# A third buffer for rows of q and k, and new slots for their loads: a threshold attention followed by a gated two-layer network

## Chip, cores and metric

One core of one Trainium2 chip. The metric is the device time of one launch in microseconds (us), as the median of several runs; the profile is of one execution of the same program.

## What is computed

Inputs are q, k and v of shape (8, 8, 576, 64) in f32 (batch, head, row, head dimension), a number tau, and two weight matrices, 512 x 2048 and 2048 x 512.

```python
scores = q @ k.T / 8
scores = where(scores >= rowmax(scores) - tau, scores, -1e9)
attn = exp(scores - rowmax(scores)); attn = attn / (sum(attn) + 1e-9)
x = (attn @ v)              # heads side by side: (4608, 512)
h = x @ w_in                # (4608, 2048)
out = (h * clip(h + 3, 0, 6) / 6) @ w_out
```

## The kernel before, in words

**Units.** The 64 heads are worked in 16 quads of four heads; a batch entry has two quads (g = 0, 1). A quad has nine slots: in slots 0 to 3 the first pair of heads, 128 rows at a time, in slots 4 to 7 the second pair, and in slot 8 the last 64 rows of all four heads. So there are 144 slots, numbered n = 0 to 143 (slot s of quad Q is n = 9Q + s), and one loop over n (lines 470 to 558) writes out by hand, for every engine, what is issued in each slot. The order of the program is the order on each engine and on each DMA queue; semaphores are added to it by the framework.

**What one slot does.** TensorE computes the scores of slot n + 1 (line 281, or 287 in slot 8). VectorE reads those of slot n out of PSUM and takes the row maxima (302). ScalarE masks (310) and, one slot later, takes the exponential and the row sums (315). GpSimd multiplies with the reciprocal sums and writes bf16 probabilities pn (323), also one slot later; in time this ends some seven to nine us after the slot's line 302 began. SyncE then issues a DMA transpose of pn (331) into pT (slots 0 to 7) or pR (slot 8). In the first 21 slots every odd one is transposed by TensorE instead (339). TensorE multiplies the transposed probabilities with v: `av_main` for the first pair in slot 8, `av_main` for the second pair in slot 3 of the next quad, `av_rest` for slot 8 in slot 4 of the next quad (348, 351). Beside this, from slot 23 on, each slot takes a piece of the two-layer network of an earlier batch entry (378, 387 or 389, 395, 407, 415), and finished output rows are stored by SyncE (428).

**Loads of q and k.** `load_quad` (80) takes tiles from `nat_pool` and appends five jobs to the list `loads`: k rows of the first pair, q rows of the first pair, the last 64 rows, k of the second pair, q of the second pair. The loop starts one job per slot (553), behind that slot's transpose on SyncE's queue. For batch entries 0 and 1 (quads 0 to 3) a k or q job is two DMAs (88), and TensorE transposes the rows. From quad 4 on a k or q job is four DMAs of 32-column blocks (97 and 92), the job of the last rows is two DMAs (124), and VectorE transposes (239, 245). Of quad Q + 1, q of the first pair is read in slot 5 of quad Q, k in slot 6, the last rows in slot 7; the second pair is read in slots 1 and 2 of its own quad. With two buffers quad Q + 2 may be loaded from slot 4 of quad Q on; that is where its jobs are appended (480). Quad 4 so falls to slots 22 to 26, quad 5 to 34 to 38, quad 6 to 40 to 44, quad 7 to 49 to 53, and each later quad nine slots after the one before it.

**Other loads.** Values of a batch entry (`load_v`, 133) are four casting DMAs issued by GpSimd from the list `vcasts`; the 32 casting DMAs of the weights stand in `casts` (156). Lines 554 to 557 say which list gets a turn in which slot: weights one per slot in slots 4 to 15, 20, 21 and 29 to 32, two per slot in 22 to 28; values of the second entry in 16 to 19, of the third in 34 to 37, and later ones as they are appended (slots 45, 63, 81, ...).

**Waits of SyncE.** All DMAs of SyncE's queue share eight completion semaphores in turn, so each DMA also waits for the one eight places before it. A transpose besides waits for its pn, a load for the readers of its buffer. What stands behind a waiting instruction of SyncE waits with it.

Of the kernel before, what the change touches and what calls it, by code (L numbers as in the profile page):

```python
# [21 lines left out]
def kernel(  # L22
# [17 lines left out]
    NQUAD = B * H // 4  # L40
# [5 lines left out]
    tau = float(tau)  # L46

    singles = ctx.enter_context(tc.tile_pool(name="singles", bufs=1))
    nat_pool = ctx.enter_context(tc.tile_pool(name="nat", bufs=2))
    v_pool = ctx.enter_context(tc.tile_pool(name="vp", bufs=2))  # L50
    qk_pool = ctx.enter_context(tc.tile_pool(name="qk", bufs=2))
    s_pool = ctx.enter_context(tc.tile_pool(name="sp", bufs=4))
# [15 lines left out]
    nat = {}  # L68
# [6 lines left out]
    casts = []  # L75
# [4 lines left out]
    def load_quad(quad):  # L80
        b, g = divmod(quad, 2)
        nat[quad] = (nat_pool.tile([P, 1152], F32, tag="nq", name="nq"),
                     nat_pool.tile([P, 4, 4, D], F32, tag="km", name="km"),
                     nat_pool.tile([P, 2 * D], F32, tag="kr", name="kr"))
        nq, km, kr = nat[quad]

        def main(dst, src, h, order, by=nc.sync):
            by.dma_start(out=dst[:, :, h, :], in_=src[b, 4 * g + h, 0:512, :].rearrange(order, t=4))

        def blocks_q(n, a, j):  # L90
            c = 32 * (2 * a + j)
            nc.sync.dma_start(out=nq[c:c + 32, n * S:(n + 1) * S].rearrange("p (k d) -> p k d", d=32),
                              in_=q[b, 4 * g + 2 * n + a, :, 32 * j:32 * j + 32].rearrange("(k r) d -> r k d", r=32))

        def blocks_k(n, a, j):
            c = 32 * (2 * a + j)
            nc.sync.dma_start(
                out=km[c:c + 32].rearrange("p t h d -> p (t h d)")[:, n * 512:(n + 1) * 512].rearrange(
                    "p (t m d) -> p t m d", t=4, d=32),
                in_=k[b, 4 * g + 2 * n + a, 0:512, 32 * j:32 * j + 32].rearrange("(m r t) d -> r t m d", r=32, t=4))  # L100

        def load_k(n):
            if b < NB:
                for a in range(2):
                    main(km, k, 2 * n + a, "(p t) d -> p t d")
            else:
                for a in range(2):
                    for j in range(2):
                        blocks_k(n, a, j)

        def load_q(n):
            if b < NB:
                for a in range(2):
                    main(nq[:, 0:1024].rearrange("p (t h d) -> p t h d", h=4, t=4), q, 2 * n + a, "(t p) d -> p t d",
                         by=nc.scalar if quad == n == 0 else nc.sync)
            else:
                for a in range(2):
                    for j in range(2):
                        blocks_q(n, a, j)

        def rest():
            for dst, src in ((kr[:], k), (nq[:, 1024:1152], q))[0:2 if b < NB else 1]:
                for n in range(2):
                    nc.sync.dma_start(out=dst[64 * n:64 * n + 64, :].rearrange("p (h d) -> p h d", h=2),
                                      in_=src[b, 4 * g + 2 * n:4 * g + 2 * n + 2, 512:S, :].rearrange("h p d -> p h d"))

        for n in range(2):
            loads.append(lambda n=n: load_k(n))
            loads.append(lambda n=n: load_q(n))
            if n == 0:  # L130
                loads.append(rest)

    def load_v(b):
        vm = v_pool.tile([P, H, 4 * D], BF16, tag="vm", name="vm")
        vr = vrs[b % 2]
        vsb[b] = (vm, vr)
        for g in range(2):
            vcasts.append(lambda g=g: nc.gpsimd.dma_start(
                out=vm[:, g * 4:g * 4 + 4, :],
                in_=v[b, g * 4:g * 4 + 4, 0:512, :].rearrange("h (p t) d -> p h (t d)", t=4)))  # L140
        for a in range(2):
            vcasts.append(lambda a=a: nc.gpsimd.dma_start(
                out=vr[a * 64:(a + 1) * 64, a, :, :],
                in_=v[b, :, 512:S, :].rearrange("(hp a) p d -> a p hp d", a=2)[a]))
# [21 lines left out]
    def start(jobs, n):  # L166
        for _ in range(min(n, len(jobs))):
            jobs.pop(0)()
# [144 lines left out]
    def sm_exp(sl, i):  # L313
        s = sl.s[:, i, :]
        nc.scalar.activation(out=s, in_=s, func=Act.Exp, accum_out=sl.rsum[:, i:i + 1])  # L315

    def sm_recip(sl):
        nc.vector.reciprocal(out=sl.rinv[:], in_=sl.rsum[:])  # L318
# [54 lines left out]
    def mm1(item, pool=None):  # L373
        b, ni, c0, w = item
        hps = (pool or ps_h).tile([P, 2, 512], F32, tag="s" if pool else "h", name="h")
        for n in range(2):
            for ki in range(KI):
                nc.tensor.matmul(hps[:, n, 0:w], w_in_sb[:, ki, (ni + n) * P:(ni + n + 1) * P],  # L378
                                 xT[b][:, ki, c0:c0 + w], start=(ki == 0), stop=(ki == KI - 1))
        return hps[:, :, 0:w]  # L380
# [89 lines left out]
    for n, sl in enumerate(queue):  # L470
        quad, slot = sl.quad, sl.slot
        b, g = divmod(quad, 2)
        now = n
        if slot in (0, 4):
            pts[2 * quad + slot // 4] = pt_pool.tile([P, 9, 512], BF16, tag="pT", name="pT")
        if slot == 8:
            ptr[quad] = ptr_pool.tile([P, 9, P], BF16, tag="pR", name="pR")
        if quad == 0 and slot == 0:
            load_quad(1)
        if slot == (4 if quad else 8) and quad + 2 < NQUAD:  # L480
            load_quad(quad + 2)
        if slot == 0 and g == 1 and b + 1 < B:
            load_v(b + 1)
        if prev is not None:
            for i in range(2):
                sm_exp(prev, i)
        sm_max(sl)

        if slot != 8 and todo1:
            item, then = todo1.pop(0)  # L490
            h = mm1(item)
            r = mm1_relu(h, on_act=(slot in ((1, 2, 3, 5, 6) if quad >= 2 * NB else (0, 1, 3, 5))))
            mm1_gate(item, h, r)
            todo2.extend(then)
        copies = pe_transpose(queue[n - 2]) if n > 1 and queue[n - 2].on_chip else None
        if prev is not None:
            sm_recip(prev)
        if copies:
            copies()
        outs = []  # L500


        pieces = 0 if slot == 3 else 1
        if slot == 0:
            second = True
        if second and slot < 2 and len(todo2) > 1 and todo2[0][1] == todo2[1][1]:
            pieces, second = 2, False
        for _ in range(pieces):
            if todo2:
                bb, mt, part = todo2.pop(0)  # L510
                mm2_part(bb, mt, part)
                if part == 3:
                    outs += mm2_out(bb, mt, on_act=False)
        for i in range(2):
            sm_mask(sl, i)
        evict = None
        nxt = 2 * quad + 2
        if slot == 1:
            evict = transpose_q(2 * quad + 1)
        elif slot == 2:  # L520
            evict = transpose_k(2 * quad + 1)
        elif n == 3:
            evict = transpose_rest(0, of_k=False)
        elif slot == 3 and quad > 0:
            av_main(2 * quad - 1)
        elif slot == 4 and quad > 0:
            av_rest(quad - 1)
            if quad % 2 == 0:
                todo1.extend(moe_of(quad // 2 - 1))
        elif slot in (5, 6, 7) and quad + 1 < NQUAD:  # L530
            if slot == 5:
                alloc_qk(quad + 1)
                evict = transpose_q(nxt)
            elif slot == 6:
                evict = transpose_k(nxt)
            else:
                evict = transpose_rest(quad + 1)
        elif slot == 8:
            av_main(2 * quad)
        if evict:  # L540
            evict()
        if n == 0:
            warm_up(8)
        if n + 1 < len(queue):
            queue[n + 1].tiles = scores(queue[n + 1].quad, queue[n + 1].slot)
        if n < 8:
            warm_up(6)
        if prev is not None:
            sm_norm(prev)
        flush()  # L550
        late.extend(outs)
        if not 30 < n < 34:
            start(loads, 1)
        if n < 4 or 15 < n < 20 or n > 33:
            start(vcasts, 1)
        elif n > 3:
            start(casts, 2 if 21 < n < 29 else 1)
        prev = sl

    for i in range(2):  # L560
# [78 lines left out]
```

## Time and profile before

| | |
|---|---|
| median of three runs | 549.75 us (549.46, 549.75, 554.11) |
| the profiled execution | 551.66 us, its span 549.9 us |
| granted TensorE clock, mean | 0.997 |
| TensorE matmul busy | 524.2 us, 95% |
| ScalarE, VectorE, GpSimd busy | 463.3 (84%), 429.1 (78%), 305.1 us (55%) |
| DMA queue of SyncE | 67.47 MB, 70.0% of the 16 engines' span |
| DMA queue of GpSimd | 8.92 MB, 13.8% |

Starts of line 302 show when slots begin. The first of a quad and the length of the quad, in us:

| quad | 0 | 1 | 2 | 3 | 4 | 5 | 6 | 7 | 8 |
|---|---|---|---|---|---|---|---|---|---|
| slot 0 begins | 9.5 | 35.2 | 60.7 | 88.2 | 123.0 | 155.1 | 187.0 | 216.9 | 248.4 |
| length | 25.7 | 25.6 | 27.4 | 34.8 | 32.1 | 31.9 | 29.9 | 31.5 | 31.2 |

In the profile PE is TensorE, PEld its weight loads, DVE VectorE, ACT ScalarE, POOL GpSimd, SP SyncE and SPq its queue of DMA issues; L12 is line 12. A timeline line gives start and length in us, engine, line, operation, output and input, how many instructions were merged, and in square brackets how long the engine had been idle and what ended that. A DMA issue's length is the time it held the issuing queue, not the transfer. A busy PE is not PE at its peak, since matmuls are pipelined.

### The profile page before, as it was taken

The page shows a single profiled execution, that of the slowest core. Times are in us where ns is not written, and L with a number is a line of the kernel's source. Part 1 is how long each engine was busy: PE and PEld are TensorE (multiplying, and loading weights), DVE is VectorE, ACT ScalarE, POOL GpSimd, SP SyncE. Part 2 cuts the span into 40 slices and gives each one's busy share as a digit, 9 for nine tenths or more (in the row PEclk, how much of TensorE's full clock was granted, in tenths as well). Part 3 has the DMA queues.
Part 4 walks back from the last instruction along what each step waited for, and adds up shares of the span by engine and source line. Part 5 has one row for each costly group of instructions (what it writes and reads, how often), then busy time and mean ns, then how long its engine had stood idle before and what let it go on. Part 6 is the DMA issues. An engine that isn't in the chain of part 4 may idle for free.

```text
span 549.9 us, 11477 instructions
## 1 busy us (share of the span) xinstructions
PE 524.2 (95%) x3733; PEld 300.5 (55%) x3774; DVE 429.1 (78%) x1055; ACT 463.3 (84%) x986; POOL 305.1 (55%) x646
## 2 busy tenths in 40 slices
PE   8999898899999999999999999999999999999997
PEld 7755455445545565555555555555555555554663
DVE  3788886688978888888989788888988788873441
ACT  3999989789989899899899899899888899993440
POOL 1888888665566555755566555754556555561000
PEclk9999999899999999999999999999999999999999
DMA  5999989969979788997789788988689785653102
GB/s 110 140 133 180 183 124 181 188 108 177 163 135 196 128 163 145 171 165 141 117 154 199 129 167 129 207 152 149 131 132 191 140 155 99 124 111 90 39 19 77
DMA packets 311692, 77.52 MB, mean 141 GB/s; under 512 B 294608, under 2 KB 307152, under 8 KB 311632
## 3 DMA queue, kind: packets, MB, share of 16 engines
q1 hardware_dynamic: 293024, 67.47, 70.0%
q0 software_dynamic: 17408, 8.92, 13.8%
q8 instruction: 30, 0.49, 0.4%
q10 hardware_dynamic: 1200, 0.39, 0.3%
q14 instruction: 30, 0.25, 0.2%
HBM read 36.70 MB, written 9.44 MB: 84 GB/s over the span
## 4 chain that ended last, share of the span: by engine, by line
PE 55%; ACT 10%; DVE 7%; DMA 5%; POOL 4%; issue 4%; SPq 1%; POOLq 0%; DVEq 0%
PE o L407 17%; PE h L378 16%; PE s L281 15%; ACT s L310 4%; PE av L348 4%; ACT s L315 3%; DVE s L302 3%; POOL pn L323 3%; DMA pR<-pn 3%; ACT r L387 2%; PE s L287 2%; DMA pT<-pn 2%; DVE g L395 1%; DVE r L389 1%; DMA km<-in_k_dram 1%
## 5 line engine op out<-in xcount | busy, mean ns | idle before, releaser
L323 POOL TENSOR_SCALAR pn<-s,rinv 128x576 bf16<-128x576 f32 x288 | 211.6, 745 | 126.7 <-DVE rinv L318 61.1
L302 DVE TENSOR_SCALAR_CACHE_REDUCE s<-s 128x576 f32<-128x576 f32 x288 | 205.3, 749 | 33.0 <-PE s L281 24.9
L310 ACT ACTIVATE s<-s,bias 128x576 f32<-128x576 f32 x288 | 206.9, 766 | 26.7 <-POOL bias L305 26.3
L315 ACT ACTIVATE s<-s 128x576 f32<-128x576 f32 x288 | 192.4, 670 | 0.3
L281 PE MATMUL s<-kT,qT 64*128 64x288 f32 x1024 | 172.8, 432 | 4.5 <-DVE s L302 4.2
L378 PE MATMUL h<-xT,w_in_sb 128*128 128x320 bf16 (+1 forms) x1024 | 145.8, 288 | 3.6 <-DVE g L395 2.2
L407 PE MATMUL o<-w_out_sb,g 128*128 128x512 bf16 x535 | 133.5, 379 | 6.0 <-DVE osb L415 3.7
L281 PEld LDWEIGHTS s<-kT,qT 64*128 64x128 f32 x1024 | 96.1, 186 | 65.9 <-DVE s L302 35.0
L378 PEld LDWEIGHTS <-w_in_sb 128*128 128x128 bf16 x1024 | 92.0, 98 | 66.9 <-issue 40.2
L395 DVE SCALAR_TENSOR_TENSOR g<-r,h 128x512 bf16<-128x512 f32 (+1 forms) x128 | 96.4, 754 | 37.2 <-ACT r L387 35.8
L305 POOL TENSOR_SCALAR bias<-m 128x1 f32<-128x1 f32 x288 | 54.4, 189 | 64.8 <-DVE s L302 44.7
L407 PEld LDWEIGHTS <-g 128*128 128x128 bf16 x576 | 55.6, 98 | 58.2 <-issue 9.7
L387 ACT ACTIVATE r<-h,three 128x640 f32<-128x640 f32 (+1 forms) x86 | 63.0, 733 | 27.0 <-PE h L378 26.6
L315 ACT ACTIVATION_READ_ACCUMULATOR s<-s 128x1 f32 x288 | 54.2, 188 | 0.0
L415 DVE TENSOR_SCALAR osb<-o 128x512 f32<-128x512 f32 x31 | 20.9, 675 | 21.7 <-PE o L407 21.4
L348 PE MATMUL av<-pT,vm 128*64 128x512 bf16 x256 | 33.7, 385 | 1.8 <-DMA pT<-pn 1.8
L348 PEld LDWEIGHTS <-vm 128*64 128x64 bf16 x512 | 17.6, 110 | 27.2 <-issue 15.8
L389 DVE TENSOR_SCALAR r<-h 128x512 f32<-128x512 f32 (+1 forms) x42 | 31.5, 750 | 0.3 <-PE h L378 0.3
L318 DVE RECIPROCAL rinv<-rsum 128x2 f32<-128x2 f32 x144 | 23.0, 160 | 8.4 <-ACT s L315 7.7
L360 DVE CAST xT<-av 128x512 bf16<-128x512 f32 x32 | 21.8, 681 | 6.5 <-PE av L351 6.5
L302 DVE DVE_READ_ACCUMULATOR s<-s 128x1 f32 x288 | 24.0, 83 | 0.0
L287 PE MATMUL s<-kT,qT 64*64 64x288 f32 x256 | 21.3, 415 | 0.6 <-DVE s L302 0.6
(57 smaller groups left out, 220.6 us busy)
## 6 DMA issues: line engine op xcount, KB each, us to landing
out_dram<-osb SPq DMA_DIRECT2D x31, 256.0 KB, 2.7
nq<-in_q_dram SPq DMA_DIRECT2D x96, 72.0 KB, 2.9
km<-in_k_dram SPq DMA_DIRECT2D x96, 64.0 KB, 2.6
vm<-in_v_dram POOLq DMA_DIRECT2D x16, 256.0 KB, 5.3
km<-in_k_dram SPq DMA_DIRECT2D x16, 128.0 KB, 3.7
w_in_sb<-in_moe_w_in_dram POOLq DMA_DIRECT2D x16, 128.0 KB, 4.1
w_out_sb<-in_moe_w_out_dram POOLq DMA_DIRECT2D x16, 128.0 KB, 4.2
pT<-pn SPq DMA_TRANSPOSE x119, 3.7
```

The costliest lines, as they stand in the source:

```text
L281: nc.tensor.matmul(tiles[a][:, hf, 0:HALF], qT_of(pair)[a * 64:(a + 1) * 64, t * P:(t + 1) * P], keys(pair, a, hf), start=True, stop=True)
L302: nc.vector.tensor_scalar(out=sl.s[:, i, :].rearrange("p (a b) -> p a b", a=2), in0=ps[:, :, 0:HALF], scalar1=1.0, scalar2=None, op0=Alu.m ...
L305: nc.gpsimd.tensor_scalar(out=sl.bias[:, i:i + 1], in0=sl.m[:, i:i + 1], scalar1=-scale, scalar2=tau, op0=Alu.mult, op1=Alu.add)
L310: nc.scalar.activation(out=s, in_=s, func=Act.Prelu, bias=sl.bias[:, i:i + 1], scale=scale, alpha=REJECT)
L315: nc.scalar.activation(out=s, in_=s, func=Act.Exp, accum_out=sl.rsum[:, i:i + 1])
L323: nc.gpsimd.tensor_scalar(out=pn[:, i, :], in0=sl.s[:, i, :], scalar1=sl.rinv[:, i:i + 1], scalar2=1.0, op0=Alu.mult, op1=Alu.mult)
L348: nc.tensor.matmul(ps[a * 64:(a + 1) * 64, :], vm[:, 2 * hp + a, c * D:(c + 1) * D], pT[:, 5 * a + c, cols], start=(c == 0), stop=False)
L378: nc.tensor.matmul(hps[:, n, 0:w], w_in_sb[:, ki, (ni + n) * P:(ni + n + 1) * P], xT[b][:, ki, c0:c0 + w], start=(ki == 0), stop=(ki == KI ...
L387: nc.scalar.activation(out=r, in_=hps, func=Act.Relu, bias=three[:])
L389: nc.vector.tensor_scalar(out=r, in0=hps, scalar1=3.0, scalar2=0.0, op0=Alu.add, op1=Alu.max)
L395: nc.vector.scalar_tensor_tensor(out=gbuf[:, ni:ni + 2, c0:c0 + w], in0=r, scalar=6.0, in1=hps, op0=Alu.min, op1=Alu.mult)
L407: nc.tensor.matmul(o_ps[0], gbuf[:, ni, mt * P:(mt + 1) * P], w_out_sb[:, ni, :], start=(ni == 0), stop=(ni == NI - 1))
```

## The change

`nat_pool` gets a third buffer, so a quad's rows may be loaded a quad earlier. Jobs of quads 1 and 2 are appended in slot 0, those of quad Q + 3 in slot 3 of quad Q. No job of `loads` starts in slots 20 to 35. By this rule quads 1 to 4 are loaded in slots 0 to 19 without a pause, quads 5 to 8 in slots 36 to 55 without a pause, quad 9 in slots 57 to 61, and each later quad in slots 3 to 7 of the quad three before it. Values of the third entry go to slots 32 to 35; weights go two per slot in slots 22 to 29 and end with slot 31. Orders of TensorE, VectorE and ScalarE are the same; on GpSimd only these casts move; SyncE has the same DMAs in another order.

```diff
-    nat_pool = ctx.enter_context(tc.tile_pool(name="nat", bufs=2))
+    nat_pool = ctx.enter_context(tc.tile_pool(name="nat", bufs=3))
...
         if quad == 0 and slot == 0:
             load_quad(1)
-        if slot == (4 if quad else 8) and quad + 2 < NQUAD:
-            load_quad(quad + 2)
+            load_quad(2)
+        if slot == 3 and quad + 3 < NQUAD:
+            load_quad(quad + 3)
...
-        if not 30 < n < 34:
+        if not 19 < n < 36:
             start(loads, 1)
-        if n < 4 or 15 < n < 20 or n > 33:
+        if n < 4 or 15 < n < 20 or n > 31:
             start(vcasts, 1)
         elif n > 3:
-            start(casts, 2 if 21 < n < 29 else 1)
+            start(casts, 2 if 21 < n < 30 else 1)
```

## The prediction

> **What bounds the kernel now.** I read the page first, then the waits, then the timeline of SyncE's queue, which is all that the change reorders.
>
> ```profile
> span 549.9 us, 11477 instructions
> ...
> PE   8999898899999999999999999999999999999997
> ...
> DMA  5999989969979788997789788988689785653102
> ```
>
> TensorE is busy nearly throughout, so time is won only where it idles or is slowed. It drops to 8 in slices 5 to 9 (55 to 137 us), where DMA stands at 9.
>
> The timeline of SyncE's queue, slots 22 to 27:
>
> ```profile
> 77.26 3.19 SPq L97 DMA_DIRECT2D km<-in_k_dram  x4
> 80.57 2.19 SPq L331 DMA_TRANSPOSE pT<-pn  x1
> 82.81 2.51 SPq L92 DMA_DIRECT2D nq<-in_q_dram  x4
> 85.42 2.10 SPq L331 DMA_TRANSPOSE pT<-pn  x1
> 87.56 2.59 SPq L124 DMA_DIRECT2D kr<-in_k_dram  x2
> 90.25 1.73 SPq L331 DMA_TRANSPOSE pT<-pn  x1
> 92.03 3.32 SPq L97 DMA_DIRECT2D km<-in_k_dram  x4
> 95.45 2.21 SPq L331 DMA_TRANSPOSE pT<-pn  x1
> 97.70 2.20 SPq L92 DMA_DIRECT2D nq<-in_q_dram  x4
> ```
>
> Each line starts where the last one ends: the queue itself is full. The transposes issued at 80.57, 85.42, 90.25 and 95.45 are those of slots 22 to 25. The timeline of all engines shows what that costs:
>
> ```profile
> 87.82 1.47 POOL L323 TENSOR_SCALAR pn<-s,rinv 128x576 bf16<-128x576 f32 x2 [0.29 <-POOL bias L305]
> ...
> 101.08 1.05 PE L348 MATMUL av<-pT,vm 128*64 128x512 bf16 x8 [1.77 <-DMA pT<-pn]
> ```
>
> Slot 25's pn was ready at 87.82 + 1.47 = 89.29; its transpose was issued 6.16 us later and landed 5.50 us after that (chain of waits), at 100.95. TensorE waited 1.77 us. The stages behind it:
>
> ```profile
> 102.00:104.00 2.00, 2.00 (x12) 0.99 (x8) 1.16 (x3) 2.00 (x5) 1.17 (x2) 0.64 1.30 194
> 104.00:106.00 2.00, 2.00 (x11) 1.23 (x10) 1.44 (x4) 0.88 (x3) 1.00 (x3) 0.51 1.11 179
> 106.00:108.00 2.00, 2.00 (x31) 1.20 (x31) 1.64 (x4) 2.00 (x5) 0.37 (x2) 1.00 0.99 194
> ```
>
> The third figure from the end is the granted clock: half speed for about 3.4 us. Slots 30 and 31 lasted 6.35 and 4.25 us by their starts of line 302, slots 32 to 35 some 3.6.
>
> Undisturbed, the queue looks like this (slots 58 to 60):
>
> ```profile
> 206.50 2.71 SPq L97 DMA_DIRECT2D km<-in_k_dram  x4
> 209.31 1.36 SPq L331 DMA_TRANSPOSE pT<-pn  x1
> 210.72 2.22 SPq L92 DMA_DIRECT2D nq<-in_q_dram  x4
> 213.04 1.30 SPq L331 DMA_TRANSPOSE pT<-pn  x1
> 214.39 1.40 SPq L124 DMA_DIRECT2D kr<-in_k_dram  x2
> ```
>
> Here is the other half: with gaps, a k job costs 2.75, a q job 2.31, the last rows 1.44, a transpose 1.38, an output store 0.62. A block quad costs 2 x 2.75 + 2 x 2.31 + 1.44 = 11.56 us of the queue.
>
> **What the Trainium skill says.** *DMA: Bandwidth & Descriptors*, section *Anatomy of one DMA*: a DMA's semaphore wait sits on the issuing sequencer before dispatch. The trace agrees: while pn is not ready the queue stands, and jobs behind it stand too. The same page, section *Issuing engines are not separate DMA queues*: DMAs of all issuers run on the same 16 engines and interleave. The trace agrees: beside two weight casts per slot the transposes above held the queue 1.73 to 2.21 us instead of 1.3, and landed after 5.1 to 7.1 us, beside 3.2 to 3.5 undisturbed. *TensorE: Matmul & The Clock Gate*, Part 1: the clock is halved after an idle window and stays so for a window of 3413 ns; the 3.4 us above agree.
>
> **The change part by part.**
>
> *Quad 4 out of slots 22 to 26.* From the transpose of slot 22 to that of slot 26 (80.57 to 100.00) the queue issued four transposes and four jobs in 19.4 us, and fell 6.6 us behind. Without jobs it issues 1.4 us per slot of 3.3, so each transpose goes out when pn is ready. DMA load falls as well; the eighth slot of double casts (29) is hidden: slots 27 and 28 carried the like. The wait of 1.77 goes, and the 1.7 us that 3.4 us at half clock cost: 3.5, which slots 30 and 31 confirm: 6.35 + 4.25 - 2 x 3.6 = 3.4. With some 0.2 from slot 28: **-3.7** (-2.5 to -5).
>
> *Quads 2 to 4 into slots 5 to 19.* Quads 2 and 3 only come three slots earlier, into slots with half the transposes; their rows lie ready well before they are read, and the buffers' last readers (quad 2 has none, quads 3 and 4 those of quads 0 and 1) are done slots before. Quad 4 in slots 15 to 19 costs the queue 11.56 + 3 x 1.4 = 15.7 us in 15.0 us (51.3 to 66.3), beside the values' casts. Slot 16's transpose (pn ready 60.6, needed 70.0, landing after 6.2 now) would be issued behind two block jobs at about 63.6 and land at about 70. **+0.5** (0 to 1.5).
>
> *Quads 5 to 8 in slots 36 to 55, quad 9 in 57 to 61.* This is what the change costs. Before, ten jobs (34 to 38, 40 to 44) were followed by four slots without. Now 25 jobs come with one free slot (56). From the transpose of slot 35 to that of slot 61 the queue has 26 x 1.38 = 35.9, five quads 5 x 11.56 = 57.8 and seven stores 7 x 0.62 = 4.3, in all 98.0 us. Slot 35's pn is ready at 127.74, slot 61's at 217.35: 89.6 us. So the queue falls 8.4 us behind even undisturbed. The fourth entry's values (four casts in slots 45 to 48) now meet running loads. The like happened in slots 34 to 37 (four jobs, four casts, 18.05 us for 16.0) and after one job in slots 44 to 47 (about 4 us too much); I take 3. Slot 61's transpose is then 11.4 us late and lands 3.7 later, 15.1 after its pn; TensorE wants it at 227.61, 10.3 after. It waits **+4.8** in all, in several waits of 1 to 2 us at slots 48 to 66 (slot 52's and 57's transposes have 11.4 and 9.3 us). Bounds: no collision and 3.4 to land, 1.5; 6 of collision, 8. Behind a late transpose stand its followers; pn has four buffers, so GpSimd is stopped too when a transpose lands 12.5 us late, and then the scores.
>
> *The clock on these waits.* Waits of 0.5 to 1.1 us on pR (at 172, 233, 296) left the clock whole, that of 1.77 did not. I count one halving, **+1.7** (0 to 5).
>
> *Later quads, loads in slots 3 to 7 instead of 4 to 8.* A transpose-only slot now precedes slot 8's transpose, and the values' casts (slots 63, 81, 99) no longer meet a job just issued. The waits on pR at 233 and 296 (1.1 and 0.5 on TensorE) should go; slot 7's transpose now stands behind five jobs instead of four and loses about 1 us of slack. **-0.9** (-1.6 to 0.5). The third entry's casts in slots 32 to 35, without loads beside them, are hidden behind a queue that has 2 us free per slot; the third buffer itself costs no instruction.
>
> Sum: -3.7 + 0.5 + 4.8 + 1.7 - 0.9 = +2.4 us on the profiled span of 549.9: 552.3. The profiled execution took 551.66 with what lies around the span; the median of the runs is 549.75. Added to that: 552.2.
>
> **Rivals.** *The queue keeps up*: the pile-up of slots 36 to 61 stays inside the slack. For it: transposes of a slot 7 usually land 3 to 6 us before they are needed, and the queue's growing lateness shrinks with each wait. Against: 98.0 us of work in 89.6. It gives -3.7 + 0.3 + 1 - 0.9 = -3.3, about 546; without the 1, 545.4. *The waits multiply*: each missed transpose between slots 48 and 66 halves the clock and values collide for 6 us. The lateness is then 8.5, three halvings 5.1: -3.7 + 0.5 + 8.5 + 5.1 - 0.5 = +9.9, 559.6. It ends slower by over 1% once waits and clock together exceed about 9.6 us (5.5 plus the 4.1 that the rest wins). For it: the waits I expect are as long as the one that did halve the clock. Against: they are short when spread. *The first stall stays*: casts alone, two per slot to slot 29, keep the transposes slow, and the change does not free slots 22 to 31: 0 + 0.5 + 4.8 + 1.7 - 0.9 = +6.1, 555.9. Against: without jobs the queue has no backlog to pass on.
>
> **How the numbers follow.** My case 0.47, its own range 549 to 556; the queue keeps up 0.18; the waits multiply 0.27; the first stall stays 0.08. A measurement of this kernel can tell about 1% from no change, 5.5 us. Under 544.25 lies only the end of the second case with a larger first gain: 0.06. Above 555.25 lie most of the third, half of the fourth and a tenth of mine: 0.35. Between: 0.59. For 8 in 10: 545.5 to 560.
>
> **What would show it.** Right: slots 30 and 31 at about 3.5 us, clock 1.00 there, transposes of slots 22 to 31 issued within 0.1 us of pn; SyncE's queue without a gap from about 124 to 230, transposes of slots 48, 52, 57 and 61 issued 6 to 11 us after pn, waits of TensorE on pT between 180 and 240; quads 8 and later without waits on pR. Wrong: lateness on the queue under 6 us at slot 61, or waits at slots 41 to 43 for the rows of quad 5, for which I see 5 us to spare.

## The result, and the profile after

| | before | changed |
|---|---|---|
| median | 549.61 us (6 runs, 548.21 to 554.11) | 566.94 us (6 runs, 565.8 to 568.69) |
| span of the profiled execution | 549.9 us | 566.9 us |
| granted TensorE clock, mean | 0.997 | 0.985 |

The ratio is 1.0306 (95% interval 1.0266 to 1.0345): slower by 3%, outside the forecast's range of 545.5 to 560 and above its most likely 552.2. The profiled execution of the changed kernel took 568.69 us, the longest of its six.

The page of the changed kernel:

```profile
span 566.9 us, 11449 instructions
...
PE   8998887999999897889999999999999999999997
...
PEclk9999998999999899979999999999999999999999
DMA  5999999996799889987779888998889555664102
...
L348 PE MATMUL av<-pT,vm 128*64 128x512 bf16 x256 | 36.2, 407 | 16.9 <-DMA pT<-pn 11.8
```

The clock row has three dips (slices 7, 13 and 14, and 18 of 40); the kernel before has one, in slice 8. Line 348, which multiplies the transposed probabilities with v, now waits 16.9 us; before it was 1.8. From the waits of the changed kernel:

```profile
PE av L348 <- DMA pT<-pn: 11.8, 4, 4.9
PE av L348 <- DMA nq<-in_q_dram: 3.1, 1, 3.1
```

The second is the same kind of wait: the transpose of slot 57 landed 0.35 us before its use.

Where the 17 us arise, by the starts of line 302 (after minus before, in us):

| at the start of slot | 9 | 27 | 36 | 54 | 63 | 72 | 135 |
|---|---|---|---|---|---|---|---|
| before | 35.2 | 88.2 | 123.0 | 187.0 | 216.9 | 248.4 | 464.8 |
| changed | 35.0 | 92.8 | 124.5 | 191.9 | 227.1 | 265.4 | 481.9 |
| difference | -0.2 | 4.6 | 1.5 | 4.9 | 10.2 | 17.0 | 17.1 |

So two places lose time: slots 15 to 26 (about 5, lost in slot 26, of which slots 27 to 35 give 3 back), and slots 45 to 71 (15.5). From slot 72 on nothing changes.

SyncE's queue in the second place (timeline of the changed kernel; start, us held):

```profile
194.20 2.65 SPq L97 DMA_DIRECT2D km<-in_k_dram  x4
196.95 1.31 SPq L331 DMA_TRANSPOSE pT<-pn  x1
198.31 2.25 SPq L92 DMA_DIRECT2D nq<-in_q_dram  x4
200.65 1.32 SPq L331 DMA_TRANSPOSE pT<-pn  x1
202.07 1.21 SPq L428 DMA_DIRECT2D out_dram<-osb  x2
203.33 1.41 SPq L124 DMA_DIRECT2D kr<-in_k_dram  x2
204.84 1.32 SPq L331 DMA_TRANSPOSE pR<-pn  x1
...
233.69 3.39 SPq L92 DMA_DIRECT2D nq<-in_q_dram  x4
237.18 2.56 SPq L331 DMA_TRANSPOSE pT<-pn  x1
```

Each line begins within 0.1 us of the end of the one before it. The transposes at 196.95 and 200.65 are those of slots 51 and 52, whose pn was ready at 186.24 and 189.06: 10.7 and 11.6 us late, although these lines hold the queue no longer than undisturbed ones. The last line is slot 61's, 12.15 us late. TensorE waits for it, and the clock falls (timeline, then the stages):

```profile
243.09 1.92 PE L348 MATMUL av<-pT,vm 128*64 128x512 bf16 x8 [4.41 <-DMA pT<-pn]
```

```profile
240.00:242.00 2.00, 0.00 (x0) 0.00 (x0) 0.76 (x2) 2.00 (x4) 0.19 (x1) 1.00 1.33 190
242.00:244.00 2.00, 0.92 (x6) 0.52 (x8) 0.00 (x0) 0.94 (x4) 0.86 (x2) 0.58 1.41 253
244.00:246.00 2.00, 2.00 (x10) 0.84 (x8) 0.53 (x1) 0.00 (x0) 1.19 (x2) 0.50 1.08 260
246.00:248.00 2.00, 2.00 (x11) 0.97 (x8) 0.39 (x2) 0.00 (x0) 0.00 (x0) 0.50 1.10 159
```

TensorE is empty for 2 us and more (second figure), then works at half clock (third from the end) for 6.8 us in all. The first place looks alike, 4.87 us for slot 21's transpose in slot 26:

```profile
88.59 1.84 PE L348 MATMUL av<-pT,vm 128*64 128x512 bf16 x8 [4.87 <-DMA pT<-pn]
```

### The profile page after: what moved, and what is told of

Same layout as the page of the kernel before. It is cut to its first block, busy times and chain, and to the rows that moved or that the text cites. A ratio compares the mean times of both kernels' runs of the same rounds, so it can differ in the third digit from the quotient of the medians.

```text
span 566.9 us, 11449 instructions
## 1 busy us (share of the span) xinstructions
PE 529.7 (93%) x3733; PEld 304.0 (54%) x3774; DVE 429.7 (76%) x1055; ACT 463.1 (82%) x986; POOL 305.1 (54%) x646
## 3 DMA queue, kind: packets, MB, share of 16 engines
q0 software_dynamic: 17408, 8.92, 13.8%
## 4 chain that ended last, share of the span: by engine, by line
PE 54%; ACT 8%; DVE 6%; DMA 4%; issue 4%; POOL 3%; SPq 1%; POOLq 0%; DVEq 0%
PE h L378 16%; PE o L407 16%; PE s L281 15%; PE av L348 4%; DMA pT<-pn 3%; ACT s L310 3%; ACT s L315 3%; DVE s L302 2%; ACT r L387 2%; POOL pn L323 2%; PE s L287 1%; PE av L351 1%; DVE r L389 1%; DVE g L395 1%; DMA nq<-in_q_dram 1%
## 5 line engine op out<-in xcount | busy, mean ns | idle before, releaser
L281 PEld LDWEIGHTS s<-kT,qT 64*128 64x128 f32 x1024 | 97.4, 189 | 65.8 <-DVE s L302 32.5
L395 DVE SCALAR_TENSOR_TENSOR g<-r,h 128x512 bf16<-128x512 f32 (+1 forms) x128 | 96.4, 754 | 36.7 <-ACT r L387 35.2
L348 PE MATMUL av<-pT,vm 128*64 128x512 bf16 x256 | 36.2, 407 | 16.9 <-DMA pT<-pn 11.8
L348 PEld LDWEIGHTS <-vm 128*64 128x64 bf16 x512 | 18.8, 112 | 40.6 <-issue 32.5
```

What stands on the lines that cost most here:

```text
L281: nc.tensor.matmul(tiles[a][:, hf, 0:HALF], qT_of(pair)[a * 64:(a + 1) * 64, t * P:(t + 1) * P], keys(pair, a, hf), start=True, stop=True)
L348: nc.tensor.matmul(ps[a * 64:(a + 1) * 64, :], vm[:, 2 * hp + a, c * D:(c + 1) * D], pT[:, 5 * a + c, cols], start=(c == 0), stop=False)
L395: nc.vector.scalar_tensor_tensor(out=gbuf[:, ni:ni + 2, c0:c0 + w], in0=r, scalar=6.0, in1=hps, op0=Alu.min, op1=Alu.mult)
```

## The experiments

The theory (A) is that SyncE's queue issues more than a slot's time of work in every load slot, so that lateness grows with the number of load slots in a row, until transposes miss their use. Its rivals: the third buffer itself (B), the 16 DMA engines rather than the issuing (C), and the clock's halvings (D). "Late" below is from the end of a slot's pn on GpSimd (line 323) to the issue of its transpose.

### The third buffer alone

```diff
-    nat_pool = ctx.enter_context(tc.tile_pool(name="nat", bufs=2))
+    nat_pool = ctx.enter_context(tc.tile_pool(name="nat", bufs=3))
```

> The kernel before with a third buffer for the rows of q and k and nothing else. If the order on SyncE's queue is what costs time (theory A): within 1 us of before, 549 to 551 us. If the buffer itself costs, by where it lies or by waits that it moves (theory B): a good part of the 17 us, 555 or more.

Measured: 549.74 us against 549.87, ratio 0.9985 (0.9971 to 1.0). Theory B falls. Its profile has the waits of before: TensorE waits 1.72 us for slot 25's transpose (before 1.77).

### The early half alone

```diff
-        if slot == 3 and quad + 3 < NQUAD:
+        if slot == 3 and quad < 2:
             load_quad(quad + 3)
+        if slot == 4 and quad > 2 and quad + 2 < NQUAD:
+            load_quad(quad + 2)
...
-        if not 19 < n < 36:
+        if not 19 < n < 34:
```

> The early half of the change: third buffer, quads 1 to 4 in slots 0 to 19, none from 20 to 33, the new cast slots; quads 5 and later as before (slots 34 to 38, 40 to 44, 49 to 53, ...). The traces of before and after differ by +4.8 us at slot 27 and by +1.6 at slot 36. Theory A: 550.5 to 552.5 us, a wait of about 5 us at slot 26, none at slot 30. If the early half is what the forecast said, a gain: 546.5.

Measured: 550.75 us against 549.87, ratio 0.9997 (0.9971 to 1.0023). The early half wins nothing and loses nothing that can be told. In its profile slot 21's transpose lands 0.25 us before its use in slot 26, TensorE waits 2.47 us there (about 5 was expected), and one window at half clock goes with it, while slot 30 is better: the wait has moved from slot 30 to slot 26. How long that wait is differs between executions. Six profiles have the same program up to slot 36 but for the loads of quad 5: this one, the changed kernel's, and those of four runs below (values left out, more issues, TensorE kept busy, two pauses). In them the wait in slot 26 is 0.7 to 4.9 us, and slots 9 to 35 take 87.0 to 89.4 us, beside 87.8 before and 88.4 with the third buffer alone. The changed kernel's profile is the longest of the six, so the table above shows the early part at its worst.

### The late half alone

```diff
-        if slot == (4 if quad else 8) and quad + 2 < NQUAD:
+        if slot == (4 if quad else 8) and quad < 3:
             load_quad(quad + 2)
+        if slot == 3 and quad == 3:
+            load_quad(5)
+        if slot == 3 and 2 < quad and quad + 3 < NQUAD:
+            load_quad(quad + 3)
...
-        if not 30 < n < 34:
+        if not 26 < n < 36:
```

(from the kernel before, with the third buffer.)

> The late half: third buffer, quads 1 to 4 and all casts as before, quads 5 to 8 in slots 36 to 55 without a pause and later ones as in the changed kernel. Theory A: all of the waits at slots 53 to 66 come from this run of loads: 563 to 567 us. If early lateness or the moved casts set it off: under 558.

Measured: 564.48 us, ratio 1.0253 (1.0212 to 1.0294). This is where the time goes: 14.6 of the 17 us. Its waits of TensorE in the late part are those of the changed kernel: the transposes of slots 48, 52, 57 and 61 land 0.1 to 0.4 us before their use. The list of waits puts them down to whatever signalled last, so one kind of wait stands under several names (2.2 of the first 6.5 us are the early wait on slot 25's transpose, as before the change):

```profile
PE av L348 <- DMA pT<-pn: 6.5, 2, 4.3
PE av L348 <- DMA nq<-in_q_dram: 3.0, 1, 3.0
PE av L348 <- ACT s L310: 2.5, 1, 2.5
```

### The same loads, spread out

```diff
-        if not 19 < n < 36:
+        if n < 15 or slot % 2 == 0 and not 21 < n < 30:
```

> The changed kernel with the same loads spread out: one job in each of the first 15 slots, from then on only in even slots of a quad (five in nine slots), none in 22 to 29. Same bytes, same issues, same third buffer. Theory A: the queue keeps up, lateness under 4 us everywhere, no half clock: 545 to 550 us. If the loads' number or the third buffer costs whatever the order: near 560 or more.

Measured: 548.15 us, ratio 0.996 (0.9939 to 0.9981): 0.4% faster than before, with the changed kernel's buffers, bytes and number of DMAs. Its queue in the stretch that failed above:

```profile
203.66 2.24 SPq L92 DMA_DIRECT2D nq<-in_q_dram  x4
206.01 3.57 SPq L331 DMA_TRANSPOSE pT<-pn  x2
209.63 2.66 SPq L97 DMA_DIRECT2D km<-in_k_dram  x4
212.39 1.34 SPq L331 DMA_TRANSPOSE pT<-pn  x1
213.84 0.89 SPq L428 DMA_DIRECT2D out_dram<-osb  x1
214.82 1.30 SPq L331 DMA_TRANSPOSE pT<-pn  x1
```

After a job come two transposes: 3.57 us for two that need 2.7, so the queue waits for pn there. From slot 25 on the transposes read for their uses (slots 3, 7 and 8 of each quad up to slot 71) are at most 1.9 us late and land 4 us or more before it. What counts is the order, not the amount. The early part is not clean in this order either: slot 21's transpose lands 0.25 us before its use, TensorE waits 1.29 us for it, and there is one window at half clock 7 us later, where none was expected.

### Fewer transfers in the run: the fourth entry's values left out

```diff
-            load_v(b + 1)
+            if b + 1 == 3:
+                vsb[3] = vsb[1]
+            else:
+                load_v(b + 1)
```

> The changed kernel without the four casting DMAs of the fourth entry's values (slots 45 to 48); the second entry's are used in their place, so this part of the output is another. It asks how much of the lateness of the run of loads is the collision with these casts, put at 3 us in the forecast. From slot 44's transpose to slot 48's the queue took 18.9 us in the changed kernel, 15 by the undisturbed prices. Collision: about 4 us less, 562 to 564 us. If the casts do not matter and only the number of issues does: 566 to 567.

Measured: 560.97 us, ratio 1.0211 (1.0189 to 1.0234), 6 us under the changed kernel and a little under both expectations. The queue took 104.5 us from slot 35's transpose to slot 61's, beside 107.9 in the changed kernel; slots 36 to 71 took 137.3 us beside 141.0. So about 3.5 of the 6 us belong to that stretch, near the 4 expected; the rest, by the profiles, lies in the early part, which the edit does not touch and which varies. The collision is real and not the main thing.

### More issues, the same bytes

```diff
-            nc.sync.dma_start(out=nq[c:c + 32, n * S:(n + 1) * S].rearrange("p (k d) -> p k d", d=32),
-                              in_=q[b, 4 * g + 2 * n + a, :, 32 * j:32 * j + 32].rearrange("(k r) d -> r k d", r=32))
+            for k0, k1 in ((0, 9), (9, 18)) if 4 < quad < 10 else ((0, 18),):
+                nc.sync.dma_start(out=nq[c:c + 32, n * S + 32 * k0:n * S + 32 * k1].rearrange("p (k d) -> p k d", d=32),
+                                  in_=q[b, 4 * g + 2 * n + a, 32 * k0:32 * k1, 32 * j:32 * j + 32].rearrange(
+                                      "(k r) d -> r k d", r=32))
```

> The changed kernel with each q DMA of quads 5 to 9 cut in two: 40 DMAs more in slots 37 to 61, the same bytes in the same pieces of 128 B. If issuing on SyncE's queue sets the pace (theory A): 40 x 0.55 = 22 us more of queue work, nearly all of it seen, 583 to 592 us. If the 16 DMA engines set it (theory C): no change, 565 to 569.

Measured: 581.43 us, ratio 1.0594 (1.055 to 1.0638): 14.5 us over the changed kernel, less than the 22 expected and far from none. The line numbers of this kernel are two higher:

```profile
199.68 2.65 SPq L99 DMA_DIRECT2D km<-in_k_dram  x4
202.44 1.31 SPq L333 DMA_TRANSPOSE pT<-pn  x1
203.79 4.12 SPq L93 DMA_DIRECT2D nq<-in_q_dram  x8
208.01 1.30 SPq L333 DMA_TRANSPOSE pT<-pn  x1
```

A q job of eight holds the queue 4.12 us, one of four 2.25: an issue costs about 0.5 us whether it moves 36 or 72 KB. From slot 35's transpose to slot 61's the queue took 124.4 us, 16.5 more than the changed kernel, and the total grew by 14.5. Theory C falls as the main cause: the bytes were the same, and the 16 DMA engines had less to do the later the queue ran. Their busy share from 131 to 237 us is 0.99 before, 0.90 in the changed kernel and 0.79 here.

### TensorE kept busy while it waits

```diff
         ps = bank("av")
+        if now in (53, 57, 62, 66):
+            for _ in range(12):
+                nc.tensor.matmul(ps[:], w_in_sb[:, 0, 0:P], w_in_sb[:, 0, 0:512], start=True, stop=True)
         av(ps[:], pair, pts[pair], slice(0, 512))
```

> The changed kernel with twelve matmuls of 128 x 512 on weights ahead of av_main in slots 53, 57, 62 and 66, whose result is overwritten: TensorE works while it waits there for the transposes. The trace of the changed kernel has half clock for 13.7 us in that stretch. If half clock adds to the time (theory D): 560 to 563 us. If the queue sets the pace and the clock is hidden behind it, all but the halving after the last wait: 564.5 to 567.

Measured: 562.69 us, ratio 1.0236 (1.0218 to 1.0254), 4.2 us under the changed kernel, within what was expected if half clock adds to the time, though near its upper end. The stages of this kernel:

```profile
150.00:200.00 50.00, 47.98 (x327) 26.60 (x327) 39.53 (x99) 42.47 (x94) 28.33 (x59) 1.00 0.98 149
200.00:260.00 60.00, 57.33 (x412) 31.30 (x411) 42.98 (x107) 46.70 (x101) 30.30 (x64) 1.00 0.96 160
```

The clock is 1.00 throughout, where the changed kernel has 13.7 us at half. The queue took 107.2 us from slot 35's transpose to slot 61's, as before the edit (107.9): inside the run the clock is hidden behind the queue. Slots 36 to 71 took 137.1 us instead of 141.0, and quad 7, in which the last and longest wait of this stretch lies, 35.4 instead of 38.4: after that wait no lateness covers half a clock. So D is a part, about 4 us, and mostly of the last halving, which was two windows long. This is net of what the added matmuls cost themselves (slot 57 lasts 6.15 us instead of 4.80). The 11.7 us by which slots 36 to 71 are still longer than before (125.4) stand with the clock whole.

### Two pauses in the run

```diff
-        if not 19 < n < 36:
+        if not (19 < n < 36 or 45 < n < 50 or 59 < n < 64):
```

> The changed kernel with two pauses of four slots: quads 5 and 6 in slots 36 to 45, 7 and 8 in 50 to 59, the next from 64 on; the fourth entry's values (45 to 48) fall in the first pause. If lateness grows with the length of a run of load slots (theory A): it stays under 6 us, the waits at slots 53 to 66 go, and what is left is the early half and short waits on pR: 550 to 554 us. If the late loads cost by their place or the third buffer by its use: near 560 or more.

Measured: 559.31 us, ratio 1.0188 (1.0166 to 1.0211). About two fifths of the loss is gone. The first run of ten behaves as expected: slots 52 and 53 are 3.1 and 3.8 us late, no wait at slots 53 to 57. The second starts with that lateness and ends 8.6 us late at slot 59; four slots without loads do not clear it before the fifth entry's values (slots 63 to 66) slow the transposes of slots 61 and 62, which land 6.9 and 7.3 us after their issue. TensorE waits in slot 66:

```profile
229.48 1.92 PE L348 MATMUL av<-pT,vm 128*64 128x512 bf16 x8 [2.64 <-DMA pT<-pn]
```

The same happens in slot 84 (3.37 us) with the sixth entry's. There the edit made a new dense run: quads 9 to 11 are loaded in slots 64 to 79 with one slot free. So slots 36 to 71 took 129.7 us (before 125.4, changed 141.0), but slots 72 to 134 took 3.6 us more than in either. Lateness does grow with the run, but runs of ten with pauses of four are still too dense, and what is late meets the next transfers.

### The early collision: the second entry's values moved

```diff
         if quad == 0 and slot == 0:
+            load_v(1)
             load_quad(1)
...
-        if slot == 0 and g == 1 and b + 1 < B:
+        if slot == 0 and g == 1 and 0 < b < B - 1:
...
-        if n < 4 or 15 < n < 20 or n > 31:
+        if n < 8 or n > 31:
```

(from the early half.)

> The early half of the change with the second entry's values moved from slots 16 to 19, where quad 4 is now loaded, to slots 4 to 7; weights one per slot in 8 to 21, as many as before. In the changed kernel slot 16's transpose was issued 5.7 us after its pn and slots 18 to 21 stayed as late, beside these casts. If the collision of casts and loads makes that lateness: slot 21's transpose lands over 2 us before its use, no wait at slot 26, 546 to 548.5 us. If the queue's issues alone make it (15.7 us of work in 15.0): as the early half, 550 to 551.5.

Measured: 549.89 us against 549.5, ratio 1.0018 (1.0001 to 1.0035). No gain: slot 16's transpose is 5.9 us late as before (5.7), with weight casts beside it instead of values. In this profile it is slot 16's transpose that is missed, in slot 21, and the clock stays at half for 10.2 us; this execution took 555.77 us, 5.9 above the median. So it is not the values in particular that make slots 15 to 21 late. Since the weights' casts took their place there, this run cannot tell casts beside loads from loads alone.

The same move in the spread order:

> The spread order with the same move of the second entry's values. If casts beside loads are what is left to win: 545.5 to 547.5 us. If nothing but the spread order counts: 548, as that run.

Measured: 548.2 us, ratio 0.9974 (0.9965 to 0.9982). As the spread run.

### The spread order with later double casts

```diff
-        if not 19 < n < 36:
+        if n < 15 or (slot % 2 == 0 or n == 21) and not 21 < n < 32:
...
-            start(casts, 2 if 21 < n < 30 else 1)
+            start(casts, 2 if 23 < n < 32 else 1)
```

> The spread order with the weights' double slots moved from 22 to 29 to 24 to 31, no load in 22 to 31, a load in slot 21. In the spread run the transpose of slot 21 landed 0.25 us before its use, after 7.35 us beside the first double casts and a load, and the clock was halved once behind it. Theory A with that collision: the wait and the halving go, 544.5 to 547.5 us. If the casts beside it did not matter: as the spread run, 548.

Measured: 548.63 us, ratio 0.9984 (0.9976 to 0.9992). No better than the spread run, although the wait itself is gone: slot 21's transpose lands 1.82 us before its use. One half-clock window is in the profile again, earlier, at 63 us, where no wait of TensorE before it is over 0.93 us. What is left in slots 15 to 30 was not found.

## Why the prediction was wrong

**What bounds it.** Right: the queue of SyncE, transposes behind load jobs, TensorE's wait and a halved clock. The changed kernel fails by the mechanism that the forecast priced, at the places it named (slots 48 to 66). What failed is the size of the terms, the late run of loads above all. Three readings of the kernel before were off without bearing on that: PE stands at 8 in slices 5, 7 and 8 (55 to 69 and 82 to 110 us) and not in all of slices 5 to 9; by the forecast's own prices, what the queue issued in slots 34 to 37 is 15.4 us of work, not 16.0; and of the transposes of a slot 7 only 8 of 15 land over 3 us before their use, the others 0.1 to 2.3 (slot 61's 0.16).

**Quad 4 out of slots 22 to 26, -3.7 (-2.5 to -5).** Right in kind, too large. Transposes of slots 25 to 35 left within 0.03 us of pn, and slots 27 to 35 won 3.2 us in the changed kernel's profile. About 1 of these is slot 27 catching up after the long wait (2.40 us; 3.39 before). In the spread run with the values moved, which has no half clock and no wait of over a us in this part, slots 27 to 35 take 32.8 us instead of 34.8: 2.1 won. The forecast took 3.6 us as the undisturbed length of slots 30 and 31; there they last 4.95 and 3.10, so 2.55 and not 3.4 can be won in them.

**Quads 2 to 4 into slots 5 to 19, +0.5 (0 to 1.5).** Failed. I priced the issues at undisturbed length, 15.7 us in 15.0, and looked at slot 16 alone. From slot 14's transpose to slot 21's the queue took 25.3 us (56.28 to 81.59) for four transposes and five jobs worth 4 x 1.38 + 11.56 = 17.1. That slot 16's landed 0.04 us before its use, at the 70 us of the forecast, is luck: it was issued 5.7 us late where I had 3.0, and landed after 3.8 us where I had 6.2. Slots 18, 20 and 21 stayed 5.7 to 7.1 us late, and slot 21's has little time, because these early slots are short: 8 us from pn to use before. That cost 4.8 us in the changed kernel's profile and 1.0 to 3.6 in the five others with this early part; by its own run the early half nets nothing where I had -3.2. What stretches the issues there stays open. It is not the values in particular; casts of any kind, and DMA engines that are full (their share from 56 to 66 us is 1.32; packets overlap, so it can pass 1), were not separated.

**Quads 5 to 8 in 36 to 55, quad 9 in 57 to 61, +4.8 (1.5 to 8).** The step that failed most, by its size. The sum was 98.0 us of queue work and 3 for a collision; the queue took 107.9 (slot 35's issue at 129.23 to slot 61's at 237.18). Landing took 5.8 us where I had 3.7. So 9.9 - 3 = 6.9 and 2.1 were missing: 4.8 + 6.9 + 2.1 = 13.8. Measured against the use before, moved by the 1.5 us of slot 35's later pn: 243.09 - (227.61 + 1.47) = 14.0. The transposes of slots 48, 52, 57 and 61 were 8.1, 11.6, 8.6 and 12.2 us late, where 6 to 11 was the sign of being right. Of the 9.9 us, by kind, 4.6 are in the q jobs (27.7 us for ten, 23.1 by the forecast's price), 4.1 in the transposes, 0.9 in the k jobs and the rest in stores and last rows. The medians are near the forecast's prices; single issues are what grew: 40 q DMAs held the queue 634 ns each in the mean and 517 in the median, up to 1.78 us; transposes 1.47 us in the mean and 1.35 in the median, up to 3.1. Without the fourth entry's casts 3.4 of the 9.9 are gone. What stretches the other 6.5 stays open: that lateness itself brings transposes beside later casts (slots 60 and 61 beside the fifth entry's values, 5.9 and 5.8 us to land) fits the run with pauses, where slots 61 and 62 took 6.9 and 7.3, but two transposes of 2.1 us, at 209 and 226 us, had no cast beside them.

**The clock, +1.7 (0 to 5).** Under-sized, within its range: 4.2 us by the run with TensorE kept busy. The waits of that stretch were not several of 1 to 2 us but 1.2 to 4.4, and the last went with two windows at half clock. The idle window of 3.4 us that the prediction cites was no threshold here: the clock was halved with shorter waits (1.77 us before the change, 2.14 in the changed kernel).

**Later quads, -0.9.** Failed: nothing (17.0 at slot 72, 17.1 at slot 135). The wait on pR in slot 85 did go, and the slot lasts 3.3 us instead of 3.9; slot 86 then lasts 3.5 instead of 3.0. So half a us less of this wait shortened nothing behind it; what held slot 86 stays open.

**The rivals.** That the waits multiply (559.6, with a late part of +8.5 and three halvings) was the nearest in kind; it had the halved clock about right (5.1 us) and the lateness still too small by 5 us. In the range, the upper end of each term was set from single collisions seen in the kernel before, where the queue had pauses in which to recover.

## What to carry to other kernels

SyncE's queue had a price per issue here, so a change that packs issues together must be tested against the slot's length over the whole run. About 4.2 us of issues in slots of 3.4 us (107.9 and 89.6 us over 26 slots) left transposes 12 us late after 25 jobs, while five jobs in a row, as in the later quads, cost nothing. Prices from quiet stretches were a floor: in a full queue collisions no longer get a pause to drain in, so an estimate of lateness should carry the stretched lengths (here some 10% on top), not one collision. And where the same loads went mattered more than how early they could start: one in every second slot turned +3.1% into -0.4%. Whether that order needs the third buffer was not run; from quad 5 on it starts a quad's loads in slot 6 two quads ahead, which two buffers allow.

## What the runs showed of the hardware

The length for which a DMA held SyncE's queue hardly depended on its size: medians of 0.52 us for the q DMAs of 72 KB, 0.64 for the k blocks of 64 KB and 0.58 for output stores of 256 KB in the changed kernel's late run of loads, and 0.45 for 36 KB where the q DMAs were cut in two; a DMA transpose 1.35. Beside casts from GpSimd single issues stretched to 1.8 us (q) and 3.1 us (transpose).

The length of a wait alone did not decide whether TensorE's clock was halved. Waits of 1.77 us (before) and 2.14 to 4.87 (changed) went with one or two windows of 3.4 us at half clock, one of 2.49 (early half, values moved) with three. In the run with two pauses waits of 2.61 and 3.37 us went with none. Three profiles (late half, more issues, late double casts) have a window at 63 us with no wait of over 0.93 us in the 20 us before it. Twelve matmuls placed in each of four waits kept the clock whole in that stretch.
